# Two of ten rounding operations per weight matrix unit, moved from ScalarE to VectorE in six of eight units

## Chip, cores, metric

One core of a Trainium2 chip. The metric is the device time of one execution in microseconds (us); with one core, the slowest core is that core.

## The reference, cut to what matters

A causal convolution of 7 taps per head, then a SiLU feed-forward block, in float32. The weights `w_in` and `w_out` arrive as float64.

```python
x : (8, 4096, 192) float32          # tokens, 32768 in all
w_in : (192, 2048) float64          w_out : (2048, 192) float64
y = conv(x, softmax(weight))        # 7 taps, causal, per head
h = y @ w_in
g = h * (1.0 / (1.0 + np.exp(-h)))
out = (g @ w_out).astype(np.float32)
```

## The kernel before

Tokens go in 32 blocks of 1024. Block 0 is special: it is computed while the weights are still being loaded and rounded from float64 to float32. The rounding works on the two 32-bit words of each number; there are eight units, four of `w_in` (0 to 3) and four of `w_out` (4 to 7). `vec` is VectorE, whose instructions keep their program order; ScalarE's are placed by the scheduler of the program.

```python
def rounded(dst, key):
    words = raws.pop(key).rearrange("p (n t) -> p n t", t=2)
    lo, hi = words[:, :, 0], words[:, :, 1]
    two = tpool.tile([P, 4 * TB], I32, tag="t", name="two")
    ex, st = two[:, 0:WC], two[:, WC : 2 * WC]              # 128 x 768 each
    # ... mh, one
    vec.tensor_single_scalar(ex, hi, 0x7FF * one, op=ALU.bitwise_and)
    vec.tensor_single_scalar(st, lo, 0xFF, op=ALU.bitwise_and)
    vec.tensor_scalar(ex, ex, ..., op0=ALU.max, op1=ALU.min)
    nc.scalar.sign(st, st)                                       # line 186
    nc.scalar.activation(ex, ex, AF.Copy, bias=..., scale=8.0)   # line 187
    vec.tensor_scalar(mh, hi, ...)
    # ... four two-input operations on VectorE, the last into dst

def round_in(j):                                 # units 0 to 3
    rounded(wr[j].rearrange("p a k c -> p (a k c)"), ("i", j))
    for e in range(2):                           # the halves exchanged, into ws
        nc.scalar.dma_start(out=ws[j][R * e : R * e + R], in_=wr[j][R - R * e : 2 * R - R * e])

def round_out(q):                                # units 4 to 7
    rounded(wo[q].rearrange("p a e d -> p (a e d)"), ("o", q))

# the start
# ... convolution of block 0, with round_in(0) after its first third
round_in(1)
load_in(3, nc.gpsimd)      # unit 3's raw matrix
load(1)                    # tokens of block 1
for j in range(NJ):        # NJ = 4
    up_plain(0, j)         # 48 matmuls into all 8 PSUM banks, then 8 silus on ScalarE
    if j + 2 < NJ:
        round_in(j + 2)
        load_out(j, nc.gpsimd)
    else:
        round_out(j + 2 - NJ)
        load_out(j, nc.gpsimd)
for j in range(2, NJ):
    round_out(j)
# ... convolution of block 1, then down_plain(0): 192 matmuls (line 497)
```

Some words used below: PSUM is the memory that TensorE writes to, in eight banks; the silus read and so free the banks. The halo is the few tokens ahead of a block that its convolution also needs, copied by a DMA. The differences (`win`) are the four subtractions with which VectorE finishes the operands of a block.

Wherever a line number differs by 4 to 10 between kernels below, it is the same statement (line 367 of the kernel before is line 373 of the changed one, 497 is 503, 403 is 409, 377 is 383, 211 is 217). The sign is line 186 before and 187 in the changed kernel, the copy 187 and 188.

Of the kernel before, what the change touches and what calls it, by code (L numbers as in the profile page):

```python
# [11 lines left out]
AF = mybir.ActivationFunctionType  # L12
ALU = mybir.AluOpType
# [4 lines left out]
def kernel(  # L18
# [24 lines left out]
    nc = tc.nc  # L43
# [67 lines left out]
    vec = Pinned(nc.vector)  # L111
# [36 lines left out]
    wr = [const.tile([P, 2, NK, P], F32, name=f"wr{j}") for j in range(NJ)]  # L148
    ws = [const.tile([P, 2, NK, P], F32, name=f"ws{j}") for j in range(NJ)]
    wo = [const.tile([P, 2, 2, D], F32, name=f"wo{j}") for j in range(NJ)]  # L150
# [18 lines left out]
        for a in range(2):  # L169
            queue.dma_start(out=raw[:, a, :, :], in_=out32[a, q])  # L170

    def rounded(dst, key):
        words = raws.pop(key).rearrange("p (n t) -> p n t", t=2)
        lo, hi = words[:, :, 0], words[:, :, 1]
        two = tpool.tile([P, 4 * TB], I32, tag="t", name="two")
        ex, st = two[:, 0:WC], two[:, WC : 2 * WC]
        mh = xpool.tile([P, 3 * TB], I32, tag="cmb", name="mh")[:, 0:WC]
        one = 1 << 20


        vec.tensor_single_scalar(ex, hi, 0x7FF * one, op=ALU.bitwise_and)
        vec.tensor_single_scalar(st, lo, 0xFF, op=ALU.bitwise_and)
        vec.tensor_scalar(
            ex, ex, scalar1=float(896 * one), scalar2=float(1151 * one), op0=ALU.max, op1=ALU.min
        )
        nc.scalar.sign(st, st)  # L186
        nc.scalar.activation(ex, ex, AF.Copy, bias=-float(896 * 8 * one), scale=8.0)
        vec.tensor_scalar(
            mh, hi, scalar1=one - 1, scalar2=one, op0=ALU.bitwise_and, op1=ALU.bitwise_or
        )  # L190


        vec.scalar_tensor_tensor(
            out=st, in0=lo, scalar=8, in1=st, op0=ALU.logical_shift_right, op1=ALU.bitwise_or
        )
        m = mh.bitcast(F32)
        vec.scalar_tensor_tensor(
            out=m, in0=mh, scalar=float(1 << 24), in1=st, op0=ALU.mult, op1=ALU.add
        )
        vec.scalar_tensor_tensor(  # L200
            out=ex, in0=hi, scalar=-(1 << 31), in1=ex, op0=ALU.bitwise_and, op1=ALU.bitwise_or
        )
        vec.scalar_tensor_tensor(
            out=dst, in0=m, scalar=2.0**-44, in1=ex.bitcast(F32), op0=ALU.mult, op1=ALU.mult
        )

    def round_in(j):
        rounded(wr[j].rearrange("p a k c -> p (a k c)"), ("i", j))

        for e in range(2):  # L210
            nc.scalar.dma_start(
                out=ws[j][R * e : R * e + R], in_=wr[j][R - R * e : 2 * R - R * e]
            )

    def round_out(q):
        rounded(wo[q].rearrange("p a e d -> p (a e d)"), ("o", q))

    def comb(out, u, v, op):
        nc.gpsimd.tensor_tensor(out, u, v, op=op)
# [57 lines left out]
    for k in range(NK):  # L277
# [4 lines left out]
            op=ALU.mult,  # L282
# [324 lines left out]
    for k in range(NK):  # L607
        turn_in(0, k)
        for i in range(K):
            conv(0, k, i)  # L610
        spread(0, k)
        if k == 0:
            round_in(0)
            load_in(2, nc.gpsimd)
    round_in(1)
    load_in(3, nc.gpsimd)
    load(1)
    for j in range(NJ):
        up_plain(0, j)
# [8 lines that stand above are left out]
# [56 lines left out]
```

## Time and profile before

| what | before |
|---|---|
| time, median of 3 runs | 2495.68 us (2495.47 to 2496.77) |
| TensorE busy | 98% of the span |
| start of TensorE's unbroken run (line 497) | 89.5 us |
| end of VectorE's rounding | 86.6 us |
| VectorE idle before it needs block 0's result | 21.9 us |

How to read it: from line 497 on TensorE never waits, so the profiled span is the moment at which this run starts plus a constant of some 2404 us. Only the first 90 us can be won or lost.

### The profile page before, as it was taken

How to read it: one execution, taken by the hardware profiler on the slowest of the kernel's cores; microseconds unless marked ns; L12 is line 12 of the kernel's file. 1: busy time of each engine (PE TensorE's matmuls, PEld its weight loads, DVE VectorE, ACT ScalarE, POOL GpSimd, SP SyncE). 2: the span in 40 equal slices, each digit the busy share in tenths (PEclk: the TensorE clock that was granted, in tenths of full speed). 3: DMA queues.
4: the chain of work that ended last, by engine and by line, in shares of the span. 5: the costliest groups of instructions: out<-in, count | busy, mean ns of one | idle time of the engine just before them, and what ended most of it. 6: DMA issues, size and time to landing. Idle time of an engine off the chain costs nothing.

```text
span 2493.8 us, 29780 instructions
## 1 busy us (share of the span) xinstructions
PE 2450.4 (98%) x11296; PEld 956.8 (38%) x11296; DVE 2038.6 (82%) x2736; ACT 976.7 (39%) x1759; POOL 74.1 (3%) x107
## 2 busy tenths in 40 slices
PE   5899999999999999999999999999999999999998
PEld 2343333344333443333443334333334433334432
DVE  7778888988888888889888889888888888898875
ACT  2244333444333443333443334443334433344432
POOL 4300000000000000000000000000000000000000
PEclk9999999999999999999999999999999999999999
DMA  7312222211222112222122221222221222221110
GB/s 141 76 31 42 43 52 43 43 35 35 51 51 40 38 35 43 51 43 47 31 37 49 51 43 38 38 36 52 46 44 32 41 43 51 43 43 35 35 39 13
DMA packets 450271, 110.78 MB, mean 44 GB/s; under 512 B 422305, under 2 KB 423969, under 8 KB 450129
## 3 DMA queue, kind: packets, MB, share of 16 engines
q1 hardware_dynamic: 444272, 101.26, 21.3%
q0 software_dynamic: 1600, 4.92, 0.7%
q10 hardware_dynamic: 4256, 2.72, 0.6%
q8 instruction: 88, 1.44, 0.2%
q14 instruction: 55, 0.44, 0.1%
HBM read 31.49 MB, written 25.17 MB: 23 GB/s over the span
## 4 chain that ended last, share of the span: by engine, by line
PE 96%; DVE 3%; ACT 0%; DMA 0%; issue 0%; ACTq 0%; POOL 0%; POOLq 0%; DVEq 0%
PE ps L403 47%; PE ps L458 47%; PE ps L497 2%; DVE two L109 1%; DVE nat L317 0%; DVE mh L109 0%; DMA nat<-in_x_dram 0%; PE ps L367 0%; ACT g L377 0%; DVE wr L109 0%; DVE xt L297 0%; DVE wo L109 0%; ACT two L186 0%; DVE nat L314 0%; DVE u L544 0%
## 5 line engine op out<-in xcount | busy, mean ns | idle before, releaser
L458 PE MATMUL ps<-g,wo 128*64 128x512 f32 x2976 | 873.2, 593 | 0.0
L403 PE MATMUL ps<-dup,ws 64*128 64x512 f32 x2480 | 870.0, 589 | 0.0
L427 DVE TENSOR_TENSOR g<-u,ps 128x512 f32<-128x512 f32 x744 | 488.5, 680 | 116.7 <-PE ps L403 103.0
L403 PE MATMUL ps<-win,wr 64*128 64x512 f32 x1488 | 567.9, 589 | 0.0
L458 PEld LDWEIGHTS ps<-g,wo 128*64 128x64 f32 x2976 | 275.6, 137 | 572.2 <-issue 548.7
L424 ACT ACTIVATE g<-g 128x512 f32<-128x512 f32 x744 | 445.6, 631 | 88.4 <-DVE g L427 88.4
L403 PEld LDWEIGHTS ps<-dup,ws 64*128 64x128 f32 x2480 | 362.8, 187 | 292.1 <-issue 284.3
L458 PE MATMUL ps<-t,wx 128*64 128x512 f32 x992 | 466.1, 592 | 0.0
L317 DVE SCALAR_TENSOR_TENSOR nat<-xt,taps,nat 128x512 f32<-128x512 f32 x576 | 431.4, 749 | 11.9
L541 ACT COPY cmb<-ps 64x512 f32<-64x512 f32 (+1 forms) x93 | 54.0, 581 | 965.1 <-PE ps L458 964.4
L403 PE MATMUL ps<-dup,wr 64*128 64x512 f32 x992 | 419.9, 596 | 0.0
L418 ACT COPY u<-ps 128x512 f32<-128x512 f32 x496 | 277.9, 589 | 233.4 <-PE ps L403 233.1
L458 PE MATMUL ps<-t,wo 128*64 128x512 f32 x992 | 360.5, 592 | 0.0
L444 DVE TENSOR_TENSOR t<-g,t 128x1024 f32<-128x1024 f32 x248 | 303.6, 1224 | 60.7 <-PE ps L458 50.2
L403 PEld LDWEIGHTS ps<-win,wr 64*128 64x128 f32 x1488 | 233.2, 187 | 175.7 <-issue 146.8
L444 DVE TENSOR_TENSOR t<-g 128x1024 f32<-128x1024 f32 x248 | 299.3, 1218 | 0.0
L403 PE MATMUL ps<-win,ws 64*128 64x512 f32 x496 | 242.2, 589 | 0.0
L458 PE MATMUL ps<-g,wx 128*64 128x512 f32 x496 | 233.1, 592 | 0.0
L403 PEld LDWEIGHTS ps<-dup,wr 64*128 64x128 f32 x992 | 160.5, 187 | 127.4 <-issue 119.8
L418 DVE COPY u<-ps 128x512 f32<-128x512 f32 x248 | 166.3, 680 | 11.9 <-PE ps L403 8.3
L422 ACT ACTIVATE g<-ps 128x512 f32<-128x512 f32 x248 | 143.9, 596 | 79.5 <-PE ps L403 75.6
L553 DVE STREAM_TRANSPOSE osb<-cmb 128x512 f32<-128x512 f32 x96 | 67.5, 704 | 101.9 <-ACT cmb L541 79.0
(57 smaller groups left out, 1102.2 us busy)
## 6 DMA issues: line engine op xcount, KB each, us to landing
dup<-nat SPq DMA_DIRECT2D x384, 128.0 KB, 2.3
nat<-in_x_dram SPq DMA_DIRECT2D x382, 64.0 KB, 2.5
out_dram<-osb SPq DMA_DIRECT2D x378, 64.0 KB, 1.9
raw<-in_moe_w_out_dram POOLq DMA_DIRECT2D x8, 384.0 KB, 4.4
raw<-in_moe_w_in_dram POOLq DMA_DIRECT2D x8, 192.0 KB, 5.7
ws<-wr ACTq DMA_DIRECT2D x8, 192.0 KB, 3.8
raw<-in_moe_w_in_dram ACTq DMA_DIRECT2D x4, 192.0 KB, 6.0
raw<-in_moe_w_in_dram SPq DMA_DIRECT2D x4, 192.0 KB, 3.7
```

Source lines behind the costliest of these rows:

```text
L109: return lambda *args, **kw: pin(getattr(self.engine, name)(*args, **kw))
L317: nc.vector.scalar_tensor_tensor(out=dst, in0=src, scalar=tap, in1=dst, op0=ALU.mult, op1=ALU.add)
L403: nc.tensor.matmul(bk[b, m, bn], rows(w, half), rows(v, half), start=first, stop=True, skip_group_check=True,)
L418: pin(copy(u, bk[b, m, "1"]))
L422: pin(nc.scalar.activation(g, bk[b, m, "1"], AF.Silu))
L424: pin(nc.scalar.activation(g, g, AF.Silu))
L427: pin(nc.vector.tensor_tensor(g, us.pop((b, m, i)), bk[b, m, bn], op=ALU.add))
L444: pin(nc.vector.tensor_tensor(t[i // 2][:, i % 2, :], u, v, op=ALU.subtract))
L458: nc.tensor.matmul(accs[b][i][R * half : R * half + R, :], lhs, rhs, start=first and j == 0, stop=j == NJ - 1, skip_group_check=True,)
L497: nc.tensor.matmul(acc[k][R * n : R * n + R, :], wo[j][:, a, e, R * k : R * k + R], gs[b, j, a][:, n, e, :], start=j == 0 and a == 0 and e ...
L541: pin(nc.scalar.copy(*copies[name]()))
L553: nc.vector.transpose(osb[:, i, :, :].rearrange("p k c -> p (k c)"), cmbs[b][0][:, i, :])
```

## The change

The intent: from unit 2 on, rounding shall not cross from VectorE to ScalarE and back. Sign of a number from 0 to 255 becomes a minimum with 1; the scaled copy becomes a subtraction and a multiplication in one operation.

```diff
-    def rounded(dst, key):
+    def rounded(dst, key, shared):
...
-        nc.scalar.sign(st, st)
-        nc.scalar.activation(ex, ex, AF.Copy, bias=-float(896 * 8 * one), scale=8.0)
+        if shared:
+            nc.scalar.sign(st, st)
+            nc.scalar.activation(ex, ex, AF.Copy, bias=-float(896 * 8 * one), scale=8.0)
+        else:
+            vec.tensor_single_scalar(st, st, 1, op=ALU.min)
+            vec.tensor_scalar(
+                ex, ex, scalar1=float(896 * one), scalar2=8.0, op0=ALU.subtract, op1=ALU.mult
+            )
...
     def round_in(j):
-        rounded(wr[j].rearrange("p a k c -> p (a k c)"), ("i", j))
+        rounded(wr[j].rearrange("p a k c -> p (a k c)"), ("i", j), j < 2)
...
     def round_out(q):
-        rounded(wo[q].rearrange("p a e d -> p (a e d)"), ("o", q))
+        rounded(wo[q].rearrange("p a e d -> p (a e d)"), ("o", q), False)
```

## The prediction

> **What bounds the kernel now.** I read the page first: busy shares and the chain that ended last.
>
> ```profile
> PE 2450.4 (98%) x11296; PEld 956.8 (38%) x11296; DVE 2038.6 (82%) x2736; ACT 976.7 (39%) x1759; POOL 74.1 (3%) x107
> ...
> PE 96%; DVE 3%; ACT 0%; DMA 0%; issue 0%; ACTq 0%; POOL 0%; POOLq 0%; DVEq 0%
> ```
>
> TensorE carries the end. The windows view shows it busy 76.00 of 76.00 us in each steady block of tokens, and from 100 to 300 us the list of waits has none of TensorE's. So a change before that point moves the end one for one with the moment at which TensorE starts its unbroken run, and the rounding (eight units, all before 87 us) can matter only there. Next, TensorE's timeline of the prologue (start, length, and in brackets the idle time before it and who ended it). Line 367 is the first block's up projection, four groups j=0..3 of 48 matmuls; line 497 is its down projection, 192 matmuls.
>
> ```profile
> 43.03 13.55 PE L367 MATMUL ps<-dup,wr 64*128 64x512 f32 x52 [2.67 <-ACT g L377]
> ...
> 69.58 3.33 PE L367 MATMUL ps<-dup,wr 64*128 64x512 f32 x12 [2.31 <-ACT g L377]
> 76.64 5.67 PE L367 MATMUL ps<-dup,wr 64*128 64x512 f32 x12 [3.73 <-ACT g L377]
> 83.68 5.90 PE L367 MATMUL ps<-dup,wr 64*128 64x512 f32 x24 [1.37 <-ACT g L377]
> 89.51 41.42 PE L497 MATMUL ps<-g,wo 128*64 128x512 f32 x192
> ```
>
> The reader is to see that the unbroken run starts at 89.51, and that before it TensorE waits for ScalarE's silu: a group fills all eight PSUM banks, so the next needs them emptied. ScalarE's timeline tells why the silus are late:
>
> ```profile
> 67.47 0.84 ACT L186 ACTIVATE two<-two 128x768 int32<-128x768 int32 x1 [3.96 <-DVE two L109]
> 68.22 0.83 ACT L187 ACTIVATE two<-two 128x768 int32<-128x768 int32 x1
> 68.95 1.06 ACT L377 ACTIVATE g<-ps 128x512 f32<-128x512 f32 x2
> 74.53 0.84 ACT L186 ACTIVATE two<-two 128x768 int32<-128x768 int32 x1 [4.51 <-DVE two L109]
> ```
>
> ScalarE runs in order. Its queue is sign, copy, two silus, sign, copy, two silus; each sign waits for the next unit's first VectorE operations, so the silus come out at the pace of the rounding, a pair every 7 us, although their banks were full long before. The waits from 38 to 95 us (waiter, total, times, longest) agree:
>
> ```profile
> ACT two L186 <- DVE two L109: 17.0, 4, 4.5
> ...
> PE ps L367 <- ACT g L377: 10.1, 4, 3.7
> ...
> DVE two L109 <- ACT two L186: 5.0, 1, 5.0
> ```
>
> The last line is the one time that VectorE waits for ScalarE: at unit 2, where the sign stands behind eight silus.
>
> **What the Trainium skill says.** "ScalarE: Activation LUTs", section "What ACT_TABLE_LOAD costs", gives an ACTIVATE with immediate scale and bias 186 + 0.833 ns per element: 826 ns for 768. The trace has medians of 844 (sign) and 828 (copy). "VectorE: DVE Perf Modes", section "The perf-mode tier table", has fp32 tensor_scalar at two elements a cycle and two-tensor operations at one. The trace agrees for 4-byte integers: 552 ns at best for the 768-element tensor_scalar, 957 for the two-input form. "SBUF — State Buffer", section "Who interferes with whom", says that a VectorE operation in a 2-port mode and a GpSimd operation block each other. GpSimd works through 49 to 83 us here, and the same tensor_scalar there takes 0.70 to 0.81 us, which fits. "TensorE: Matmul & The Clock Gate", Part 1, says that after about 3.4 us of idling the clock is halved; the trace grants 0.63 in 76.6 to 83.7 us, after the gaps of 2.31 and 3.73.
>
> **The change, part by part.** The instruction order of both builds shows what moves. TensorE's is unchanged. VectorE gets two tensor_scalars more in each of units 2 to 7, right after the clamp. ScalarE loses 12 operations of units 2 to 7: 12 x 0.84 = 10 us of its work, worth nothing in itself. What counts is the new queue: eight silus, the two DMA issues of unit 2's weights (they wait for VectorE to finish unit 2), two silus, the two DMA issues of unit 3's weights (they wait for unit 3), then all 22 remaining silus with no wait for rounding. So two of the six waits stay, as DMA issues.
>
> *VectorE.* An added operation costs about 0.5 us from start to start alone, about 0.72 beside GpSimd (clamp to next operation, 58 to 83 us). Six units: 1.1 + 5 x 1.4, about 8 us.
> Unit 2 starts at 39.92, as now, without the stall of 4.95 us (51.43 - 4.95 + 1.1 = 47.6, less 0.4 because its last two operations no longer lie beside GpSimd's sums), so it ends near 47.2 rather than 51.4.
> Unit 3 then needs its raw matrix. The view of that tile says of the last two of its four DMAs, sent from GpSimd up to 41.2 us:
>
> ```profile
> L163 POOL DMA_DIRECT2D raw<-in_moe_w_in_dram x2: 612/614/617, 40.6 to 41.2; - x2
> ...
> DMA to landing us min/median/max: 7.7/8.2/8.6
> ```
>
> That is 49.8 at the latest. Today it is hidden, since unit 3 starts at 51.4; now it becomes a wait. In the new order some competing loads of tokens are sent later, so I take 48.8. Unit 3 costs 7.4 + 1.4 = 8.8 us, hence 57.6; it was 58.8.
> Unit 4's raw matrix is also sent by GpSimd, behind its four sums at 49 to 52.4 us that nothing moves, and lands at 58.0 today; unit 4 starts at 58.1, where it was 58.83.
> Units 4 to 7 took 7.2, 7.2, 7.05, 6.4 us; with 1.4 each (1.2 in the last) they end at 66.7, 75.3, 83.7, 91.3, the last 4.7 later than today's 86.6.
> Behind them come transposes (1.9), the wait for the halo (2.1), the convolution (15.4) and the differences (3.75): the next block's operands are ready at about 114.5, where it was 109.7.
>
> *ScalarE and TensorE.* Group j=1 starts at 43.03 as now and ends at 55.3; its first two silus come at 48.4, behind unit 2's DMA issues. In group j=2 the first quarter runs to 57.9. The second quarter needs j=1's second pair of silus, behind unit 3's DMA issues: 57.6 + 1.15 for the issues + 0.55 for a silu = 59.3, so TensorE waits 1.4 us. From there silus (0.5 us each from start to start) are faster than the matmuls (a pair per 2.6 us), and all is bound by TensorE. A group takes 48 x 0.2135 = 10.25 us at the full clock (the 192 of line 497 take 41.4), so j=2 ends at 55.3 + 10.25 + 1.4 = 67.0 and j=3 at 77.2.
> Line 497 starts at 77.2 rather than 89.5. Its quarters need the units 4 to 7 at 77.2, 87.6, 97.9, 108.3; they are ready at 66.7 to 91.3.
> It ends at 118.6, and the next block's operands are there at 114.5: 4 us to spare, where 21 were.
>
> *Sum.* 89.5 - 77.2 = 12.3 us earlier. A cross-check: today 46.5 us pass from 43.0 to 89.5 for three groups that need 30.75 at the full clock, so 15.7 are lost in gaps and at the half clock; about 2.0 of them (a half clock at 44 to 48 us) stay, and 1.4 come new. All of it lies on the path. 2495.7 - 12.3 is about **2483.5 us**, 0.5% faster.
>
> **The rivals.**
> *The DMA issue takes the sign's place.* ScalarE still stands behind unit 3's end. If the raw matrix lands at 49.8 or GpSimd blocks more of the added operations, unit 3 ends at today's 58.8 or a bit later, TensorE waits 2.6 us or more and its clock may dip once: gain 9 to 11, time 2485 to 2487. For it: the landing times. Against: only one such wait is left.
> *VectorE becomes the bound.* With 8 us more work and 5 us less stall its chain ends near 114.5. If the added operations cost 1.2 us each beside GpSimd (the two-input ones reach that), 5 to 6 us more, operands come after 118.6 and the next block starts late, or its first transposes are late behind them: time 2485 to 2490. For it: the slack drops from 21 to 4 us. Against: the same kind of operation was never over 0.96 us in the trace.
> *It is hidden anyway.* Time 2495. Against: TensorE's gaps lie straight ahead of an unbroken run, and no later wait absorbs them.
> *No wait at all.* If the raw matrix comes by 47.3, unit 3 ends at 56.1, TensorE is not stopped after 43 us: 13.7 us gained, 2482.
> *Slower* needs VectorE's chain to end after 131, 16 us later than I put it; I see no source for it.
>
> **Range and chances.** The first two rivals push up by 2 to 6 us, the fourth down by 1.5; the three runs before span 1.3 us. Hence 2480.5 to 2489.5. A gain of 2% would be 50 us, and all of TensorE's time before 89.5 us has not so much idle in it (about 33 us, of which 21 are before its first matmul). Faster 0.01, within 2% 0.98, slower 0.01.
>
> **What would show it right or wrong.** In the new profile: ScalarE's silus in one run after about 59 us, two DMA issues ahead of them; VectorE with no wait for ScalarE after unit 1, but a new wait for a DMA of the raw matrix before unit 3 (1 to 3 us); one gap of TensorE of 0 to 3 us near 58 us, none between 60 us and the down projection, no half clock at 76 us; line 497 starting at 76 to 80 us; VectorE's rounding ending near 91; no wait of TensorE at the start of the second block (about 118 us). The prediction is wrong if TensorE waits there for VectorE's differences, or if line 497 starts after 82.

## More of the kernel before

The lines are shown in the prediction; one more is used later, from VectorE's timeline of the kernel before (start, length, operation, and in brackets the idle time before it with the releaser):

```profile
131.59 0.71 DVE L553 STREAM_TRANSPOSE osb<-cmb 128x512 f32<-128x512 f32 x1 [21.91 <-ACT cmb L510]
```

Before this operation VectorE had been idle for 21.91 us: its preparation of block 1 was done long before TensorE came to it.

## The result, and the profile after

The changed kernel takes 2484.28 us (median of 4 runs, 2484.13 to 2486.81) where the kernel before takes 2495.57 (4 runs, 2495.10 to 2496.77). The ratio is 0.9956, with a 95% interval of 0.9939 to 0.9974. Ratios here and below are from the runs of both kernels in the same rounds, so not quite the ratio of the quoted medians. The interval excludes 1: a real gain of 11.3 us in medians.

The page of the changed kernel, its busy shares and its chain:

```profile
PE 2444.7 (98%) x11296; PEld 955.3 (38%) x11296; DVE 2043.7 (82%) x2748; ACT 968.8 (39%) x1747; POOL 69.9 (3%) x107
...
PE 97%; DVE 1%; DMA 1%; issue 0%; POOL 0%; ACTq 0%; ACT 0%; POOLq 0%; DVEq 0%
```

VectorE has 12 instructions more and ScalarE 12 fewer, as the diff says. VectorE's part of the chain falls from 3% to 1%; that is the rounding that had paced the silus.

TensorE's timeline of the changed kernel, the up projection of block 0 (line 373) and its down projection (line 503):

```profile
42.93 15.32 PE L373 MATMUL ps<-dup,wr 64*128 64x512 f32 x60 [2.51 <-ACT g L383]
59.61 18.78 PE L373 MATMUL ps<-dup,wr 64*128 64x512 f32 x84 [1.35 <-ACT g L383]
78.31 41.42 PE L503 MATMUL ps<-g,wo 128*64 128x512 f32 x192
```

One gap of 1.35 us has taken the place of those of 2.31, 3.73 and 1.37 us, and the unbroken run starts at 78.31 rather than 89.51: 11.2 us, the whole of the gain. The windows view, one stretch in each kernel (its length, then for TensorE, its weight loads, VectorE, ScalarE and GpSimd the busy time and in brackets the number of instructions, then the granted clock, the DMA share and GB/s), the kernel before first:

```profile
76.60:83.70 7.10, 5.69 (x13) 3.64 (x13) 7.03 (x9) 2.61 (x5) 3.85 (x5) 0.63 0.01 2
```

```profile
76.60:83.70 7.10, 7.10 (x35) 2.45 (x33) 7.03 (x10) 1.09 (x2) 2.18 (x5) 1.00 0.14 55
```

In the kernel before, 13 matmuls fall into these 7.1 us and the clock is 0.63; after, 35 do, at the full clock. So beside the gaps themselves the slow clock behind them had cost time.

ScalarE's timeline after:

```profile
46.81 1.12 ACTq L217 DMA_DIRECT2D ws<-wr  x2
47.97 1.09 ACT L383 ACTIVATE g<-ps 128x512 f32<-128x512 f32 x2 [1.67 <-PE ps L373]
57.79 1.12 ACTq L217 DMA_DIRECT2D ws<-wr  x2
58.96 5.00 ACT L383 ACTIVATE g<-ps 128x512 f32<-128x512 f32 x10 [9.90 <-DVE two L109]
```

Two silus, then 9.90 us of nothing although TensorE fills further banks in that time, because the next thing in the queue is unit 3's pair of DMA issues, and those wait for VectorE. From 58.96 on the silus run on. VectorE's timeline tells why unit 3 is late, and how much room VectorE has left at the start of block 1:

```profile
50.05 1.07 DVE L109 TENSOR_SCALAR two<-raw 128x768 int32<-128x768 int32 x2 [3.27 <-DMA raw<-in_moe_w_in_dram]
...
120.40 0.71 DVE L559 STREAM_TRANSPOSE osb<-cmb 128x512 f32<-128x512 f32 x1 [7.06 <-ACT cmb L516]
```

The stall of 4.95 us that VectorE had at unit 2 is gone, and 3.27 us of it came back as a wait for unit 3's raw matrix. At block 1 its idle time is 7.06 us where it was 21.91.

### The profile page after: what moved, and what is told of

Its sections match the earlier page's. It is cut to its first block, busy times and chain, and to the rows that moved or that the text cites. A ratio compares the mean times of both kernels' runs of the same rounds, so it can differ in the third digit from the quotient of the medians.

```text
span 2482.4 us, 29776 instructions
## 1 busy us (share of the span) xinstructions
PE 2444.7 (98%) x11296; PEld 955.3 (38%) x11296; DVE 2043.7 (82%) x2748; ACT 968.8 (39%) x1747; POOL 69.9 (3%) x107
## 4 chain that ended last, share of the span: by engine, by line
PE 97%; DVE 1%; DMA 1%; issue 0%; POOL 0%; ACTq 0%; ACT 0%; POOLq 0%; DVEq 0%
PE ps L409 47%; PE ps L464 47%; PE ps L503 2%; PE ps L373 1%; DVE two L109 0%; DVE nat L323 0%; DMA raw<-in_moe_w_in_dram 0%; DMA nat<-in_x_dram 0%; DVE mh L109 0%; DVE xt L303 0%; POOL raw L163 0%; DVE nat L320 0%; DVE u L550 0%; DVE cmb L550 0%; ACTq L217 0%
```

## The experiments

Theory A: the gain comes from the order in ScalarE's in-order queue. Silus whose banks were full stood behind signs that waited for VectorE. What is left of the wait is unit 3's DMA issues in the same queue. Rivals: B, what paid was VectorE's stall of 4.95 us at unit 2; C, what paid was 10 us of work taken off ScalarE; D, the DMA issues in ScalarE's queue are the whole trouble and the signs harmless; and that VectorE's added work is on the path, or free without bound.

All ten runs gave correct results. Each ratio is to the kernel before in the same rounds; medians of different jobs differ by up to 2.3 us for one and the same kernel (2495.41 to 2497.68 for the kernel before), so ratios and traces decide.

| run | median us | ratio to before (95%) | down projection starts |
|---|---|---|---|
| before | 2495.57 | 1 | 89.51 |
| the change | 2484.28 | 0.9956 (0.9939 to 0.9974) | 78.31 |
| 1 unit 2 alone | 2496.49 | 0.9998 (0.9984 to 1.0012) | 89.42 |
| 2 units 4 to 7 alone | 2482.58 | 0.9942 (0.9930 to 0.9955) | 76.68 |
| 3 all eight units | 2487.63 | 0.9962 (0.9949 to 0.9976) | 81.31 |
| 4 copies issued from SyncE | 2477.49 | 0.9922 (0.9909 to 0.9936) | 70.96 |
| 5 raw matrix from SyncE | 2482.09 | 0.9944 (0.9930 to 0.9958) | 75.47 |
| 6 ScalarE kept busy | 2483.48 | 0.9949 (0.9936 to 0.9963) | 78.76 |
| 7 more VectorE work | 2486.96 | 0.9962 (0.9949 to 0.9976) | 77.91 |
| 8 before, copies from SyncE | 2496.12 | 0.9999 (0.9985 to 1.0013) | 88.27 |
| 9 the change again | 2484.15 | 0.9957 (0.9945 to 0.9970) | 78.34 |
| 10 both from SyncE | 2477.09 | 0.9925 (0.9911 to 0.9938) | 71.27 |

**1. Unit 2 alone.**

```diff
-        rounded(..., ("i", j), j < 2)
+        rounded(..., ("i", j), j != 2)
-        rounded(..., ("o", q), False)
+        rounded(..., ("o", q), True)
```

> Only unit 2's rounding is done by VectorE alone; units 3 to 7 keep the two ScalarE operations. Theory A (the silus stand in ScalarE's in-order queue behind signs that wait for VectorE; that is where the 11 us were): VectorE's stall of 4.95 us at unit 2 goes, but unit 3 then waits about 3 us for its raw matrix and the silus still come at the pace of units 4 to 7, the last sign ahead of 14 silus; the down projection of the first block starts at 88 to 90 us, the time is 2493 to 2496. Rival B (what was gained is VectorE's stall of 4.95 us at unit 2, the rest is side effect): most of the gain is there, 2484 to 2489.

No gain. The rest of the chain was earlier (VectorE's wait for ScalarE is not in the list of waits any more), and yet the down projection starts at 89.42. ScalarE's timeline of this run shows the pace:

```profile
72.22 0.84 ACT L187 ACTIVATE two<-two 128x768 int32<-128x768 int32 x1 [4.92 <-DVE two L109]
...
73.70 1.06 ACT L383 ACTIVATE g<-ps 128x512 f32<-128x512 f32 x2
78.90 0.84 ACT L187 ACTIVATE two<-two 128x768 int32<-128x768 int32 x1 [4.13 <-DVE two L109]
```

Still two silus per unit. The scheduler also moved unit 3's sign ahead of the first pair of silus, so one more pair was late at the end. Rival B falls (run 2 says so from the other side: the stall is there, and so is the gain). The median, 2496.49, lies just above the 2496 that was expected, in a job in which the kernel before had 2497.68.

**2. Units 4 to 7 alone.**

```diff
-        rounded(..., ("i", j), j < 2)
+        rounded(..., ("i", j), True)
```

> Only units 4 to 7 (the matrices of the down projection) are done by VectorE alone; units 2 and 3 keep the ScalarE operations and unit 2 its stall. Theory A: the whole gain is there: after unit 3's DMA issues (at about 60 us, as in the kernel before) 20 silus follow without a wait; group j=2 already has its second pair of silus by then, so TensorE's gap near 58 us is under 0.5 us and the down projection starts at 76.5 to 78.5; 2482.5 to 2484.5, the same as the change or 1 us better, with VectorE's stall of 5 us in place. Rival B: almost none of the gain, 2493 to 2496.

The whole gain, with two thirds of the added operations and with VectorE's stall at unit 2 in place (4.93 us in its trace). TensorE's timeline has no gap after 42.95:

```profile
42.95 33.79 PE L373 MATMUL ps<-dup,wr 64*128 64x512 f32 x144 [2.65 <-ACT g L383]
76.68 41.42 PE L503 MATMUL ps<-g,wo 128*64 128x512 f32 x192
```

It starts 1.6 us earlier than the change does. Here ScalarE's queue has a second pair of silus between unit 2's and unit 3's DMA issues (at 54.30), so TensorE already has the banks that it lacks at 58 us in the change. In time the two were not run in the same rounds; the ratios (0.9942 and 0.9956) overlap, so that this version is faster is shown by the trace of one run each, not by the times. So moving the operations in units 2 and 3 is worth nothing, or less.

**3. All eight units.**

```diff
-        rounded(..., ("i", j), j < 2)
+        rounded(..., ("i", j), False)
```

> All eight units by VectorE alone, the first two as well. Those two stand ahead of TensorE's first matmuls: about 1 us more in unit 0 and 1 us in unit 1, with ScalarE idle there. Theory A: everything behind moves by 1 to 2.5 us (the raw matrix of unit 3 too, whose request waits for unit 1), less about 1.3 us as the table of the silu is loaded earlier: 2485 to 2488, slower than the change. If VectorE's time in the first two units is off the path: 2483 to 2484.5.

Slower than the change in the trace: the down projection starts 3.0 us later (81.31). The median, 2487.63, is as expected and 3.3 us longer, but it is of other rounds, and the ratios (0.9962 and 0.9956) overlap, so the times alone don't show it. TensorE's first matmul is at 22.06 (21.46 in the change), and its gap at 60 us is 3.84 us long rather than 1.35:

```profile
60.52 20.86 PE L373 MATMUL ps<-dup,wr 64*128 64x512 f32 x84 [3.84 <-ACT g L383]
```

The gap ends 0.9 us later than in the change (59.61); the other 2.1 us are lost behind it, where the same 84 matmuls take 20.86 us rather than 18.78 and the clock granted is 0.74 between 60 and 70 us (1.00 in the change). So leaving the first two units as they were is right: there ScalarE is idle and VectorE is what TensorE waits for. But most of the loss in this trace is the slow clock.

**4. The copies issued from SyncE.**

```diff
-            nc.scalar.dma_start(
+            nc.sync.dma_start(
                 out=ws[j][R * e : R * e + R], in_=wr[j][R - R * e : 2 * R - R * e]
```

> The change, with the copies of the up weights issued from SyncE's queue rather than ScalarE's. Theory A says that what is left of the wait is those DMA issues in ScalarE's queue: ScalarE then has all 32 silus in one run with no wait for the rounding and the silu table loaded early; TensorE's gaps of 2.5 us at 40 us and 1.35 us at 58 us go, the down projection starts at 73 to 75 us and ends ahead of or with VectorE's differences (113 us): 2479 to 2482. If VectorE's rounding itself (not the queue) held TensorE: 2484.

Better than expected: 2477.49 us. TensorE has no gap of ScalarE's making at all, from its timeline:

```profile
29.21 41.82 PE L373 MATMUL ps<-dup,wr 64*128 64x512 f32 x176 [2.87 <-DMA dup<-nat]
70.96 41.42 PE L503 MATMUL ps<-g,wo 128*64 128x512 f32 x192
```

The two gaps, 2.5 and 1.35 us, are 3.9 us of the 7.35. Another 1.7 us or so is the half clock that followed the first gap: in the change the clock granted was 0.81, 0.50, 0.50, 0.50 and 0.99 in the five stretches of 1 us from 43 us on (what is missing to 1.00 adds up to 1.7 us, so some 3.4 us were at half speed), here 1.00 in each. The remaining 1.8 us are not broken down. VectorE's differences end at 112.1, the down projection at 112.3: VectorE is now as late as TensorE.

**5. Unit 3's raw matrix requested from SyncE.**

```diff
-    load_in(3, nc.gpsimd)
+    load_in(3, nc.sync)
```

> The change, with unit 3's raw matrix requested from SyncE ahead of the next block's tokens, rather than from GpSimd beside them. Theory A: the last wait in ScalarE's queue (unit 3's DMA issues) is set by the landing of this matrix at 49.8 us; it lands by 45, VectorE's wait of 3.3 us ahead of unit 3 goes, the issues come at 54 to 55 us, before TensorE needs the second pair of silus (57.9), and the gap of 1.35 us goes: the down projection starts at 76.5 to 77.2, 2482.5 to 2483.3. If the landing doesn't set that gap: 2484 to 2484.6, gap as in the change.

As expected, and 1 us better. VectorE's timeline has the wait down from 3.27 to 0.49 us:

```profile
46.96 1.50 DVE L109 TENSOR_SCALAR two<-raw 128x768 int32<-128x768 int32 x2 [0.49 <-DMA raw<-in_moe_w_in_dram]
```

The DMA issues come at 54.95 rather than 57.79, and the gap of 1.35 us is gone. So that gap was set by the landing of this matrix, by way of VectorE and ScalarE's queue. The 1 us more is probably the clock: here it was 0.50 from 36 to 39 us, ahead of the gap in which TensorE waits anyway, and 1.00 behind that gap.

**6. ScalarE kept busy.** In each of units 2 to 7 a sign and a copy of the removed size on a scratch tile.

```diff
             vec.tensor_single_scalar(st, st, 1, op=ALU.min)
+            pin(nc.scalar.sign(idle, idle))
+            pin(nc.scalar.activation(idle, idle, AF.Copy, scale=8.0))
```

> The change, plus a sign and a copy of the removed size on ScalarE for each of units 2 to 7, on a scratch tile, waiting for each other but not for VectorE: ScalarE's 10 us of work are back, the waits for VectorE are not. Theory A (the waits counted, not the work): silus keep ahead of TensorE, the down projection starts within 1 us of the change's 78.3; 2484 to 2485.5. Rival C (ScalarE's time was the limit of the prologue, and the change pays by taking work off it): most of the 11 us are lost again, 2490 to 2496.

The down projection starts at 78.76 and the gain stays (0.9949). TensorE's timeline, then ScalarE's:

```profile
58.51 20.32 PE L377 MATMUL ps<-dup,wr 64*128 64x512 f32 x84 [1.89 <-ACT g L387]
78.76 41.42 PE L507 MATMUL ps<-g,wo 128*64 128x512 f32 x192
```

```profile
60.73 0.89 ACT L193 ACTIVATE idle<-idle 128x768 int32<-128x768 int32 x1
61.66 0.84 ACT L194 ACTIVATE idle<-idle 128x768 int32<-128x768 int32 x1
62.41 2.04 ACT L387 ACTIVATE g<-ps 128x512 f32<-128x512 f32 x4
```

Only six of the twelve operations stood among the silus; the other six came behind the last one. So half of the work was back where it could hold a silu, and the queue was not quite that of before. Nothing is lost, and in the kernel before ScalarE had idled 17.0 us in waits for VectorE ahead of its signs, so it was not short of time: rival C falls.

**7. More VectorE work.**

```diff
             vec.tensor_single_scalar(st, st, 1, op=ALU.min)
+            for _ in range(4 if key[0] == "o" else 0):
+                vec.tensor_single_scalar(st, st, 1, op=ALU.min)
```

> The change, with the added minimum repeated four more times in units 4 to 7 (it changes nothing in the result): 16 operations, about 12 us more on VectorE after ScalarE's queue is free. Theory A: VectorE's chain has 6.3 us to spare at the start of the second block (differences end at 113.3, the first block's down projection at 119.7), so the down projection still starts at 78.3, the second block is late by about 12 - 6.3 = 5 to 7 us, and the time is 2488 to 2491. If VectorE's added work is on the path in full: 2495 to 2497; if it is free beyond that: 2484.

Time 2486.96, better than the 2488 to 2491 expected, since the 16 operations cost 0.54 us each and not 0.75: VectorE's differences end at 121.9 where they ended at 113.3, 8.6 us later. The up projection was not touched (77.91), and block 1 started at 119.26 and took 78.53 us (block 2 starts at 197.79) where it takes 75.88 in the change (119.67 to 195.55): 2.65 us lost, 8.6 less 6.3 of room being 2.3. (The ratios, 0.9962 and 0.9956, overlap; the loss is shown by the traces.) TensorE's timeline shows where it begins:

```profile
119.26 1.55 PE L411 MATMUL ps<-dup,wr 64*128 64x512 f32 x5
...
122.40 1.13 PE L411 MATMUL ps<-dup,ws 64*128 64x512 f32 x4 [0.30 <-DMA dup<-nat]
```

What TensorE lacks there are the copies of the convolved tokens, sent behind VectorE's convolution. The bracket shows only part of the loss: in the first 10 us of block 1 it runs 43 matmuls rather than 50, and in 4.5 us from 138 us on 17 rather than 22, just behind a wait of VectorE of 2.49 us for the next halo. So VectorE's added operations are on the path when there are 8.6 us of them; that some 6 us are free is read from the trace of the change, and no run with less was made.

**8. The kernel before, with the copies issued from SyncE.** The edit of run 4, applied to the kernel before.

> The kernel before (signs and copies on ScalarE), with the copies of the up weights issued from SyncE's queue. The DMA issues no longer block ScalarE, the signs still do. Theory A: the silus still come at the pace of the rounding, though VectorE's chain is some 3 us earlier as the queue is free at unit 2; the down projection starts at 85 to 89 us: 2491 to 2495. Rival D (the blocking of ScalarE's queue by the DMA issues was the whole trouble, and the signs are harmless): 2477 to 2483.

No gain beyond noise (2494.86 to 2497.34); the down projection starts 1.2 us earlier. TensorE's gaps are there again, and ScalarE's silus stand behind the signs:

```profile
57.27 5.89 PE L367 MATMUL ps<-dup,wr 64*128 64x512 f32 x12 [3.02 <-ACT g L377]
...
70.34 6.79 PE L367 MATMUL ps<-dup,wr 64*128 64x512 f32 x14 [2.71 <-ACT g L377]
```

```profile
68.96 0.84 ACT L186 ACTIVATE two<-two 128x768 int32<-128x768 int32 x1 [4.22 <-DVE two L109]
69.71 1.06 ACT L377 ACTIVATE g<-ps 128x512 f32<-128x512 f32 x2
```

The very edit that gives the change 7 us gives the kernel before nothing. Rival D falls as the whole cause: the signs hold the silus with or without the DMA issues. The two together are what ScalarE's queue must be rid of, and the signs hide what the DMA issues are worth. (2496.12 lies above the 2491 to 2495 expected; VectorE's rounding ended 4.4 us earlier, at 82.3, but the scheduler put 15 silus behind the last sign, where the kernel before has 12.)

**9 and 10. The change again, and with both transfers from SyncE.** Run 9 is the change without an edit; run 10 has the edits of runs 4 and 5.

> The change itself once more, on the chip and in the rounds of the next kernel, for the comparison. Theory A: 2484 to 2485 where the kernel before has 2495 to 2497, a ratio of 0.9945 to 0.996; the down projection of the first block starts at 77 to 79 us.

> The change with both the copies of the up weights and unit 3's raw matrix sent from SyncE. Theory A: with the copies off ScalarE's queue nothing of the rounding holds TensorE any more (it ran from 29 to the end without a gap of ScalarE's making), so the earlier raw matrix can only take VectorE's last wait of 0.9 us and gives nothing at the end: 2476.5 to 2478.5, as with the copies alone. If VectorE's chain was what set the start of the second block there (its differences ended at 112.1, the down projection at 112.3): 1 us better, near 2476.5.

On one chip, in the same rounds: 2484.15 and 2477.09. The gain of issuing from SyncE is 7 us. The earlier raw matrix adds nothing to it, as run 4 (0.9922) and run 10 (0.9925) do not differ: TensorE waits neither for ScalarE nor for VectorE there, and VectorE's end at 111.2 rather than 112.1 is no use to it. Runs 4 and 10 beat both kernels.

## Why the prediction was right

Predicted 2483.5, measured 2484.28. The mechanism was the one told, and of the steps:

| step | predicted | measured |
|---|---|---|
| unit 2 ends on VectorE | 47.2 | 46.8 |
| unit 3 waits for its raw matrix until | 48.8 | 50.0 |
| unit 3 ends | 57.6 | 57.8 |
| TensorE's one gap near 58 us | 1.4 | 1.35 |
| line 497 (now 503) starts | 77.2 | 78.31 |
| rounding ends | 91.3 | 89.9 |
| block 1's operands on VectorE | 114.5 | 113.3 |
| TensorE reaches block 1 | 118.6 | 119.67 |

- *"Silus in one run after about 59 us, two DMA issues ahead of them"*: 58.96, behind the pair at 57.79. ScalarE's queue works strictly in order, as the Trainium skill says in "PSUM — Partial Sum Buffer", section "Engine vs sequencer instructions"; the 9.90 us of idle time ahead of full banks agree, and runs 1, 2, 6 and 8 show that the order and the waits in it, not the work, were the cause.
- *The raw matrix.* It landed at 49.8 as in the kernel before; that the new order of requests would bring it 1 us forward was wrong. It was offset: the two-input operations of unit 3 took 0.95 to 0.96 us each, not 1.09 to 1.21 as before, when GpSimd's sums ran beside them (now these fell elsewhere), and unit 3 cost 7.7 us rather than 8.8. Two errors of about 1.1 us cancelled: that the gap near 58 us came out at 1.35 where 1.4 was told is luck. That nothing moves GpSimd's four sums ahead of unit 4's raw matrix was wrong too (they ran from 48.15 rather than 49.0), without effect.
- *The cost beside GpSimd* was put a little high. The prediction read 0.70 to 0.81 us for the tensor_scalars at 49 to 83 us of the kernel before; the trace has 0.55 to 0.82 there. Units 4 to 7 took 32.1 us together rather than 33.2, so the rounding ended at 89.9 rather than 91.3.
- *The start of line 503* was put 1.1 us too early: the gap ended at 59.61 rather than 59.3, and the 84 matmuls behind it took 18.70 us to line 503 rather than 17.9. A group of 48 matmuls was set at 10.25 us; the 192 of the down projection in 41.4 us give 10.35, and the silus of the changed kernel, a pair per 2.575 us, give 10.3. Beside that, each turn from a wait to full speed costs some tenths that the working left out (behind the gap of 1.35 the second matmul starts only 0.5 us after the first, as it needs the second silu).
- *The first rival* (a DMA issue takes the sign's place) is real, and runs 4 and 5 remove it by two different routes. It cost the 1.35 us that were put in, but the same queue also held the table load and the first silus at 40 us, which the prediction took as given: that is where at least 4.2 further us lay (the gap of 2.51 and the 1.7 lost at half clock behind it) that nobody asked for.
- *The second rival* (VectorE becomes the bound) did not come; the trace of the change leaves 6.3 us of room where 4 were predicted, and in run 7 VectorE's 8.6 us more did reach TensorE.
- *"No half clock at 76 us"*: granted 1.00.

What stays open: runs of one kernel spread over up to 4 us (the change: six at 2484.0 to 2484.3, three at 2486.4 to 2487.1; the kernel before: 2495.0 to 2495.7, and 2496.5 to 2498.7), but not those of runs 4 and 10, which spread over 0.5 us. A stretch at half clock, 1.7 us lost, comes at different places: at 44 to 48 us in the traces of the change and of the kernel before, at 58 to 62 in those of runs 1 and 6, at 36 to 39 in run 5. One such stretch more or less on the path would be of about the right size. But both profiled executions of the change belong to its faster group and have the stretch at 44 to 48 us already, and no trace of a slower one was taken, so this is only a guess.

## What to carry to other kernels

In an engine that works in order, a short operation that waits for another engine costs what stands behind it, not its own time: look for full buffers whose consumer's next instruction waits for something unrelated. Moving such an operation to the engine that it would wait for paid here although that engine was the busier one, as its slack (here some 6 us, read from the trace) was not used up. DMA issues that wait for a producer are such operations too, and belong in a queue with nothing urgent behind them; but take all of the blockers out, since removing one alone may show no gain.

## What the Trainium skill lacked or had wrong

- "Perfetto Trace Analysis", section "Optimizing Scalar/DVE Operations", speaks of placing an operation by speed and by how saturated an engine is. It lacks the order of the queue: with the twelve operations put back on ScalarE (six of them among the silus) but without their waits the down projection started at 78.76 us instead of 78.31, while with the waits it started at 89.51.
- "PSUM — Partial Sum Buffer" says that ScalarE's queue is strictly in order; no page turns this into a rule for where to issue a DMA that waits for a producer, though the steps of a DMA issue that the pages list allow it to be worked out. Here such a pair held the silus behind it for 9.90 us, and taking the pairs out of ScalarE's queue gave 7 us.
- "ScalarE: Activation LUTs", section "What ACT_TABLE_LOAD costs", has 1.28 us for the load plus 1.38 for a drain, 2.66 in all. The load's 1.28 is in the traces; the drain is not: in run 4 a copy ended at 36.09, the load took 36.10 to 37.38, and the first silu started at 37.40.
- "TensorE: Matmul & The Clock Gate", Part 1, ties the half clock to a free-running window of about 3.4 us. The traces agree that the same gap need not have the same effect, and here a gap shorter than that window was enough: of two gaps at 40 us, that of the change (2.51 us) was followed by some 3.4 us at half the clock, and that of run 1 (2.65 us) by none.
